# Batch 3 of a linear-attention and MLP kernel: its attention moved from four chunks into one slot, k of batch 4 mapped a group earlier, v and q of batch 4 loaded earlier

## The chip, the cores and the metric

The kernel runs on one core of a Trainium2 chip. The metric is the time of one execution on the device in microseconds (us), the median over several runs. An engine here is one of five units of the core that run their own instruction streams in order and wait for each other by semaphores: PE (matrix multiplies), DVE (vector), ACT (activation functions and copies), POOL (here: casts and fills at the start) and SP (here: it issues loads and transposing transfers). PEld is the part of PE that loads weights.

## The reference, cut to what matters

There are 8 batches of 8 heads, 576 tokens and 64 features. Linear attention is computed first, then a two-layer MLP over all 4608 tokens:

```python
phi = lambda x: np.where(x > 0, x, np.exp(x) - 1.0) + 1.0
q_p, k_p = phi(q), phi(k)
kv  = np.einsum('bhsd,bhse->bhde', k_p, v)
z   = np.sum(k_p, axis=2)
num = np.einsum('bhsd,bhde->bhse', q_p, kv)
den = np.einsum('bhsd,bhd->bhs', q_p, z)[..., None] + 1e-06
x   = (num / den) # heads side by side: 512 features a token
out = gelu_tanh(x @ w_in) @ w_out          # 512 -> 2048 -> 512
```

## The kernel before, in words

**Groups and slots.** The MLP runs in nine groups j = 0 to 8. Groups 0 to 7 take 512 tokens of batch j each; group 8 takes the 64 tokens that every batch has left over. `iteration(j)` (L741) writes out a group as 32 or more steps: 16 steps "h", each of four 128x512 matmuls (L388) and one gelu on ACT (L398), and then 16 steps "o" of four 128x512 matmuls (L725), which finish four output tiles t = 0 to 3. Group 1 has the order 8 h, 8 o, 8 h, 8 o, so that its four output tiles are finished in slots 28, 29, 30 and 31. After step number s of group j, `run(j, s)` emits whatever `at(j, s, ...)` had registered for that slot. This is the planner: attention work for later batches is written into slots of the MLP of earlier ones by hand. The tiling framework keeps the program's order on each engine and puts in the semaphore waits.

**What attention of batch b needs.** Loads of q, k, v (fp32) into a pool of seven slots that all inputs share in rotation; a load into a slot waits until the former tenant was read. `linear_of` (DVE, L230) makes x+1 clipped at 1; `exp_of` (ACT, L222) makes exp(x) into a buffer of which there is one for q and one for k; `least_of` (DVE, L236) takes the smaller of both, which is phi. ACT needs another function table for exp than for gelu, so each round of exps is followed by `gelu_table` (L411). `least_q` also issues four transposing transfers of phi(q) on SP's queue (qt, L632). `cast_v_paired` (DVE, L241) casts v beside a column of ones. `kv_paired` (L246, matmuls L252) makes kv with 72 matmuls of 64x64 by 65. Then come n = phi(q) times kv with its denominators (matmuls), `divide` (DVE, L285 and L286), and four transposing transfers of the result x (xt, L655), which are the input of group b's h steps.

**Two ways to make n.** Batches 1 to 3 use `nab` (L299): a chunk of 128 tokens takes four matmuls of 128x128 by 130 (L268) against kv in block-diagonal form (`kvbds`, zeroed once on POOL), and one divide of eight heads in a pair of PSUM banks. Batches 2 and 3 do this chunk by chunk in four slots of an h stage (`plan_by_chunks`, L659). Batches 4 to 7 use `nab_quads` (L312) in slot 17 of group b-1: 64 matmuls of 64x64 by 65 (L325) at one go, six result blocks of 65 columns to a bank, in four banks of the rotating pool and the pair; the two blocks that are left in the pair take kv of batch b+1 (L252), and its copy (L350) follows after the last divide. The kv of these batches is kept as plain blocks (`kvs`).

**PSUM.** Six banks rotate among h, o and n tiles; the pair of banks is separate.

**Around the change, before.** For batch 3: `linear_of` of q and k in slots 24 and 25 of group 1, the exps of q and k in slot 23, kv in slot 2 of group 2 (`kv_in_pair`, L637), n by chunks in slots 4, 6, 8 and 10 of group 2. For batch 4: k is loaded at (1, 10), q and v at (1, 29), both exps at (2, 15) together with that of k of batch 5, `least_q` at (2, 17), the cast of v at (2, 20), and kv alone in slot 2 of group 3. For batch 5: k is loaded at (2, 11), q and v at (2, 23). The output tiles t = 0 and 2 of a group are copied out of PSUM by DVE, t = 1 and 3 by ACT (L686), and ACT issues the two stores of a group (L714) between its copies.

Of the kernel before, what the change touches and what calls it, by code (L numbers as in the profile page):

```python
# [9 lines left out]
BF16 = mybir.dt.bfloat16  # L10
# [5 lines left out]
def kernel(  # L16
# [16 lines left out]
    nc = tc.nc  # L33

    B, H, S, D = q.shape
    d_model, d_ff = moe_w_in.shape
    P = 128
    HP = P // 2
    C = 4
    MAIN = P * C  # L40
    REST = S - MAIN
    NP = H // 2
# [3 lines left out]
    E = D + 1  # L46
# [15 lines left out]
    pkv = ctx.enter_context(tc.tile_pool(name="pkv", bufs=1))  # L62
# [26 lines left out]
    def ld_tile(name, b):  # L89
        shape = [P, H, C * D] if name == "q" else [P, NP, J * D]  # L90
        ld[name, b] = pld.tile(shape, FP32, name=name + "_x", tag="ld")
# [10 lines left out]
    def load_q(b):  # L102
        ld_tile("q", b)
        nc.sync.dma_start(
            out=ld["q", b],
            in_=q[b, :, 0:MAIN, :].rearrange("h (p c) d -> p h (c d)", c=C),
        )

    def load_all_pairs(name, src, b):
        ld_tile(name, b)  # L110
        load_pairs(name, src, b)
# [6 lines left out]
                in_=q[2 * m + s, :, MAIN:S, :].rearrange("h p d -> p h d"),  # L118
            )

    def load_batch(b):
        load_q(b)
        load_all_pairs("k", k, b)
        load_all_pairs("v", v, b)

    w_st = {}

    def load_w_in(i, parts=1):
# [46 lines left out]
    load_w_out(2, slice(2, 4))  # L175
    load_w_out(3, slice(0, 2))
    load_w_out(3, slice(2, 4))
    load_batch(2)
    load_batch(3)

# [1 line left out]
    nc.vector.memset(warm, 0.0)  # L184
    make_identity(nc, ident)
    vps = [pkv.tile([P, J * NP, E], BF16, name=f"vp{i}") for i in range(2)]
    kvbds = [pkv.tile([P, NP, 2 * E], BF16, name=f"kvbd{i}") for i in range(4)]
    kvs = [pkv.tile([P, NP, E], BF16, name=f"kv{i}") for i in range(4)]
    for i in range(2):
        nc.gpsimd.memset(vps[i][:, :, D:E], 1.0)  # L190
    for t in kvbds:
# [23 lines left out]
    def exp_of(name, b, hs=None):  # L215
        x = ld[name, b]
        hs = hs or slice(0, x.shape[1])
        if (name, b) not in exps:
            e = name + ("_e" if name != "qr" or b % 2 else "_f")
            exps[name, b] = pe.tile([P, x.shape[2] // D, x.shape[1], D], BF16, name=e)  # L220
        o, i = maps_view(name, b, x, exps[name, b], hs)
        nc.scalar.activation(o, i, AF.Exp)  # L222
# [17 lines left out]
    def cast_v_paired(b, us, fn):  # L240
        fn(  # L241
            out=vp_paired(b)[:, :, us, 0:D].rearrange("p j u d -> p u j d"),
            in_=ld["v", b][:, us].rearrange("p u (j d) -> p u j d", d=D),
        )
# [30 lines left out]
    def kv_of_head(b, s, i):  # L275

        r = slice(HP * s, HP * (s + 1))
        return kvs[b % 4][r, i, :] if b > 3 else kvbds[b][r, i, E * s : E * (s + 1)]

    def divide(x_v, n_v):  # L280

# [11 lines left out]
    def x_tile():  # L293
        return px.tile([P, d_model], BF16, name="x")
# [4 lines left out]
    def nab(qt_c, b):  # L299
        x, n_ps = x_tile(), pair_of_banks("n_ps")  # L300
        nab_mm(qt_c, kvbds[b], [n_ps[:, a] for a in range(2)])
        divide(by_parity(x), n_ps[:, :, 0 : 4 * E].rearrange("p a (u e) -> p a u e", e=E))
        return x
# [8 lines left out]
    def nab_quads(qt_cs, bs, kv_b):  # L312

        ns = [[bank("n_ps", [P, 6 * E]) for _ in range(2)] for _ in range(2)]
        n_pair = pair_of_banks("n_ps")
        ns.append([n_pair[:, s] for s in range(2)])
        units = [(c, i, a) for c in range(C) for i in range(2) for a in range(2)]
        for n, (c, i, a) in enumerate(units):  # L320
            g = n // 6
            for t in range(2):
                for s in range(2):
                    cs = slice(HP * t, HP * (t + 1))
                    nc.tensor.matmul(  # L325
                        ns[g][s][cs, E * (n - 6 * g) : E * (n - 6 * g + 1)],
                        lhsT=qt_cs[c][HP * s : HP * (s + 1), 2 * a + i, cs],
                        rhs=kv_of_head(bs[c][t], s, 2 * a + i),
                        skip_group_check=True,
                    )  # L330
        if kv_b is not None:
            for ii in range(2):
                kv_paired(kv_b, ii, lambda a, ii: n_pair[:, a, E * (4 + ii) : E * (5 + ii)])

        def x_of(transposed):
            x = pxs.tile([P, C, d_model], BF16, name="xs")
            x_v = x.rearrange("p c (i s a d) -> p s (c i) a d", s=2, a=2, d=D)
            for g in range(2):
                for s in range(2):
                    divide(  # L340
                        x_v[:, s, 3 * g : 3 * (g + 1)],
                        ns[g][s].rearrange("p (k a e) -> p k a e", a=2, e=E),
                    )
                for c in ((0,), (1, 2))[g]:
                    transposed(c, x[:, c])
            n_v = n_pair[:, :, 0 : 4 * E].rearrange("p s (k a e) -> p s k a e", a=2, e=E)
            divide(x_v[:, :, 6:8], n_v)
            transposed(3, x[:, 3])
            if kv_b is not None:
                nc.vector.tensor_copy(  # L350
                    out=kvs[kv_b % 4].rearrange("p (a i) e -> p a i e", a=2),
                    in_=n_pair[:, :, 4 * E : 6 * E].rearrange("p a (i e) -> p a i e", e=E),
                )

        return x_of
# [24 lines left out]
            nc.tensor.transpose(t_ps[:, n, :], x[:, P * i : P * (i + 1)], ident)  # L380
        fn(out=xt_c[:, blocks.start : blocks.stop], in_=t_ps)

    xts = {}
    qts = {}

    def h_mm(h_ps, xt, m, ts=slice(0, MAIN), blocks=range(KM)):
        for c in blocks:
# [118 lines left out]
    def at(j, slot, fn, *args):  # L506


        fill.setdefault((j, slot), []).append((fn, args))
# [68 lines left out]
        at(0, 35, h_begin, b, 0, slice(0, 3 * P))  # L578
        at(0, 35, h_begin, b, 0, slice(3 * P, MAIN))

    def plan_prepare(b, s_linear, s_exp):
        def casts():
            cast_v_paired(b, slice(0, NP), nc.vector.tensor_copy)

        def exps_all():
            for n in "qk":
                exp_of(n, b)

        j, s = s_linear
        for i, n in enumerate("qk"):  # L590
            at(j, s + i, linear_of, n, b)
        at(j, s + (7 if b == 4 else 2), casts)
        j, s = s_exp
        at(j, s, exps_all)
        at(j, s + 2, least_q, b)
        at(j, s + 4, least_of, "k", b)

    def plan_prepare_late(b):

        j = b - 3  # L600
        if b == 5:
            at(j, 15, exp_of, "k", b)
            at(j, 22, linear_of, "k", b)
        else:
            at(j, 12, linear_of, "k", b)
        at(j + 1, 8 if b == 5 else 4, cast_v_paired, b, slice(0, NP), nc.vector.tensor_copy)
        at(j + 1, 13, linear_of, "q", b)
        at(j + 1, 15, exp_of, "q", b)
        if b > 5:
            at(j, 15, exp_of, "k", b)  # L610
        at(j + 1, 20, least_q, b)
        at(j, 22, least_of, "k", b)

    def plan_rest(m):
        j = 5 + m // 2
# [21 lines left out]
    def kv_in_pair(b):  # L637
        kv_ps = pair_of_banks("kv_ps")
        for ii in range(2):
            kv_paired(b, ii, lambda a, ii: kv_ps[:, a, E * ii : E * (ii + 1)])  # L640
        src = kv_ps[:, :, 0 : 2 * E].rearrange("p a (i e) -> p a i e", e=E)
        if b > 3:
            nc.vector.tensor_copy(out=kvs[b % 4].rearrange("p (a i) e -> p a i e", a=2), in_=src)
        else:
            for s in range(2):
                r = slice(HP * s, HP * (s + 1))
                nc.vector.tensor_copy(
                    out=kvbds[b][r, :, E * s : E * (s + 1)].rearrange("p (a i) e -> p a i e", a=2),
                    in_=src[r],
                )  # L650

    def transposed_x(b, c, x):
        if b not in xts:
            xts[b] = pt.tile([P, NP, MAIN], BF16, name="xt")
        nc.sync.dma_start_transpose(out=xt_chunk(b, c), in_=x)  # L655

    rest_qt = {}

    def plan_by_chunks(b, j, s_kv, s_n):  # L659
        def n(c):  # L660
            transposed_x(b, c, nab(qts[b][:, c], b))

        at(j, s_kv, kv_in_pair, b)
        for c in range(C):
            at(j, s_n + 2 * c, n, c)

    def plan_attention(b):

# [105 lines left out]
            run(j, slot)  # L774

    plan_second()
    plan_prepare(2, (1, 2), (1, 7))
    at(1, 7, gelu_table)
    plan_by_chunks(2, 1, 16, 18)
    plan_by_chunks(3, 2, 2, 4)  # L780
    at(1, 10, load_all_pairs, "k", k, 4)
    plan_prepare(3, (1, 24), (1, 23))
    at(1, 23, gelu_table)
    at(1, 29, load_q, 4)
    at(1, 29, load_all_pairs, "v", v, 4)
    at(2, 11, load_all_pairs, "k", k, 5)
    at(2, 23, load_q, 5)
    at(2, 23, load_all_pairs, "v", v, 5)
    at(3, 2, kv_in_pair, 4)
    plan_prepare(4, (2, 13), (2, 15))  # L790
    for b in range(5, B):
        plan_prepare_late(b)
    for m in range(C):
        plan_rest(m)
    for b in range(4, B + 1):
        plan_attention(b)
    for b in range(6, B):
        at(b - 3, 1, load_all_pairs, "k", k, b)
        at(b - 3, 1, load_q, b)
        at(b - 3, 1, load_all_pairs, "v", v, b)  # L800
# [38 lines left out]
```

## Time and profile before

| what | us |
|---|---|
| median of 4 runs (284.19 to 284.82) | 284.64 |
| the profiled execution | 284.82 |
| its span, first instruction to last | 283.0 |
| PE busy | 277.2 |
| ACT busy | 164.5 |
| DVE busy | 103.2 |
| POOL busy | 15.5 |

How to read it: the span is what the instructions of the core cover; 1.8 us of the profiled execution lie around it. Busy time of one engine lies beside that of the others, so the column does not add up to the span. A matmul is shown with its full latency (379 ns for a 128x512 one), but the next one starts long before it ends; the space from start to start is what a matmul costs PE.

### The profile page before, as it was taken

Reading aid. Unit: us, or ns where it says so; the run is one execution under the profiler, and the core shown is the slowest. Engines: PE = TensorE matmul, PEld = TensorE weight load, DVE = VectorE, ACT = ScalarE, POOL = GpSimd, SP = SyncE. Lnnn points to the kernel's source line nnn. Section 1 sums busy time; section 2 is a strip of 40 time slices with the busy share of each in tenths; the row PEclk is TensorE's granted clock in tenths of the full one; section 3 lists DMA queues with packets and bytes.
Section 4 is the critical chain, followed back from the end, with each engine's and each line's share of the span. In section 5 each row is a group of like instructions: output and inputs, shape, how many; then the busy total and the mean of one; then the engine's idle time right before and its main releaser. Section 6 shows DMA issues by size and latency. Waiting matters only on the chain.

```text
span 283.0 us, 5377 instructions
## 1 busy us (share of the span) xinstructions
PE 277.2 (98%) x2293; PEld 135.9 (48%) x2293; DVE 103.2 (36%) x176; ACT 164.5 (58%) x224; POOL 15.5 (5%) x22
## 2 busy tenths in 40 slices
PE   8899999999999999999999999999999999999995
PEld 3484455445454444454445444544444444444444
DVE  2850286435856280286124650260115001400001
ACT  4768878785966955692468336832682264026400
POOL 4047200000000000000000000000000000000000
PEclk9999999999999999999999999999999999999999
DMA  6999999977899849966894660056505300420022
GB/s 234 400 407 396 411 401 404 402 254 209 90 207 332 225 90 330 398 226 167 172 393 111 164 132 0 2 148 142 120 2 139 120 2 0 138 87 0 0 76 74
DMA packets 59591, 53.83 MB, mean 190 GB/s; under 512 B 35760, under 2 KB 45360, under 8 KB 59568
## 3 DMA queue, kind: packets, MB, share of 16 engines
q1 hardware_dynamic: 56784, 44.58, 52.1%
q10 hardware_dynamic: 2784, 8.91, 8.5%
q8 instruction: 18, 0.29, 0.4%
q14 instruction: 5, 0.04, 0.0%
HBM read 36.70 MB, written 9.44 MB: 163 GB/s over the span
## 4 chain that ended last, share of the span: by engine, by line
PE 94%; DMA 3%; SPq 1%; DVE 1%; issue 0%; ACT 0%
PE o_ps L725 44%; PE h_ps L388 44%; DMA v_x<-in_v_dram 3%; PE n_ps L325 1%; PE kv_ps L252 1%; PE n_ps L268 1%; PE n_ps L252 1%; PE t_ps L380 1%; SPq L95 1%; SPq L100 0%; PE t_ps L534 0%; DVE vp L241 0%; DVE x L370 0%; DVE kvbd L264 0%; DVE o_sb L686 0%
## 5 line engine op out<-in xcount | busy, mean ns | idle before, releaser
L725 PE MATMUL o_ps<-w_out_sb,g 128*128 128x512 bf16 (+2 forms) x608 | 128.2, 368 | 0.0
L388 PE MATMUL h_ps<-xt,w_in_sb 128*128 128x512 bf16 (+1 forms) x564 | 114.6, 359 | 0.0
L398 ACT ACTIVATE g<-h_ps 128x512 bf16<-128x512 f32 x144 | 84.7, 599 | 38.9 <-PE h_ps L388 36.7
L388 PEld LDWEIGHTS <-w_in_sb 128*128 128x128 bf16 x628 | 58.3, 98 | 63.5
L725 PEld LDWEIGHTS <-g 128*128 128x128 bf16 x608 | 57.5, 98 | 63.6
L686 ACT COPY o_sb<-o_ps 128x512 f32<-128x512 f32 (+1 forms) x19 | 10.8, 576 | 61.8 <-PE o_ps L725 53.9
L686 DVE COPY o_sb<-o_ps 128x512 f32<-128x512 f32 (+1 forms) x19 | 12.2, 644 | 47.8 <-PE o_ps L725 42.9
L285 DVE RECIPROCAL r<-n_ps 128x6 f32<-128x6 f32 (+2 forms) x42 | 8.1, 193 | 55.5 <-PE n_ps L325 45.8
L222 ACT ACTIVATE k_e<-k_x 128x2304 bf16<-128x2304 f32 (+1 forms) x9 | 17.1, 1901 | 2.4 <-DVE k_p L236 1.4
L222 ACT ACTIVATE q_e<-q_x 128x2048 bf16<-128x2048 f32 (+1 forms) x9 | 15.5, 1721 | 3.4 <-DMA q_x<-in_q_dram 3.3
L230 DVE TENSOR_SCALAR k_p<-k_x 128x2304 bf16<-128x2304 f32 (+1 forms) x9 | 11.0, 1221 | 17.0 <-DMA k_x<-in_k_dram 17.0
L286 DVE TENSOR_TENSOR xs<-n_ps,r 128x384 bf16<-128x384 f32 (+1 forms) x25 | 14.6, 584 | 0.9
L230 DVE TENSOR_SCALAR q_p<-q_x 128x2048 bf16<-128x2048 f32 (+1 forms) x9 | 9.9, 1102 | 13.5 <-DMA q_x<-in_q_dram 13.5
L236 DVE TENSOR_TENSOR q_p<-q_p,q_e 128x2048 bf16<-128x2048 bf16 (+1 forms) x9 | 9.9, 1101 | 11.7 <-ACT q_e L222 11.6
L388 PE MATMUL h_ps<-xt_rest,w_in_sb 128*128 128x512 bf16 x64 | 14.0, 379 | 0.0
L241 DVE CAST vp<-v_x 128x2304 bf16<-128x2304 f32 (+1 forms) x9 | 11.0, 1226 | 7.2 <-DMA v_x<-in_v_dram 7.0
L411 ACT ACT_TABLE_LOAD x9 | 11.5, 1283 | 0.2
L236 DVE TENSOR_TENSOR k_p<-k_p,k_e 128x2304 bf16<-128x2304 bf16 (+1 forms) x9 | 11.0, 1221 | 1.3 <-ACT k_e L222 1.0
L420 PE MATMUL w_ps<-warm 128*128 128x512 bf16 x32 | 10.2, 478 | 1.2 <-DVE warm L184 1.2
L286 DVE TENSOR_TENSOR x<-n_ps,r 128x512 bf16<-128x512 f32 (+1 forms) x17 | 10.7, 628 | 0.6
L222 ACT ACT_TABLE_LOAD x8 | 10.3, 1283 | 0.1
L144 POOL CAST w_in_sb<-w_st 128x512 bf16<-128x512 f32 (+2 forms) x6 | 7.6, 1269 | 14.9 <-DMA w_st<-in_moe_w_in_dram 14.9
(50 smaller groups left out, 79.7 us busy)
## 6 DMA issues: line engine op xcount, KB each, us to landing
out_dram<-o_sb ACTq DMA_DIRECT2D x16, 512.0 KB, 3.1
k_x<-in_k_dram SPq DMA_DIRECT2D x7, 1152.0 KB, 11.5
v_x<-in_v_dram SPq DMA_DIRECT2D x7, 1152.0 KB, 12.9
q_x<-in_q_dram SPq DMA_DIRECT2D x6, 1024.0 KB, 12.7
w_st<-in_moe_w_in_dram SPq DMA_DIRECT2D x3, 1024.0 KB, 13.6
q_x<-in_q_dram SPq DMA_DIRECT2D x4, 512.0 KB, 8.9
w_st<-in_moe_w_out_dram SPq DMA_DIRECT2D x2, 1024.0 KB, 12.5
w_st<-in_moe_w_out_dram SPq DMA_DIRECT2D x4, 512.0 KB, 11.2
```

The costliest lines, as they stand in the source:

```text
L222: nc.scalar.activation(o, i, AF.Exp)
L230: nc.vector.tensor_scalar(o, i, 1.0, 1.0, op0=ALU.add, op1=ALU.max)
L236: nc.vector.tensor_tensor(p, p, e, op=ALU.min)
L241: fn(out=vp_paired(b)[:, :, us, 0:D].rearrange("p j u d -> p u j d"), in_=ld["v", b][:, us].rearrange("p u (j d) -> p u j d", d=D),)
L285: nc.vector.reciprocal(r, n_v[heads + (D,)])
L286: nc.vector.tensor_tensor(x_v, n_v[heads + (slice(0, D),)], r[heads + (None,)].to_broadcast(shape + [D]), op=ALU.mult,)
L388: nc.tensor.matmul(h_ps[:, ts], lhsT=w_in_sb[:, c, P * m : P * (m + 1)], rhs=xt[:, c, ts], start=(c == 0), stop=(c == KM - 1), skip_group_ ...
L398: nc.scalar.activation(g[:, m, :], h_ps, AF.Gelu_apprx_tanh)
L411: nc.scalar.preload_act_table_set("gelu_apprx_tanh_and_others")
L420: nc.tensor.matmul(w_ps, lhsT=warm[:, 0:P], rhs=warm)
L686: (nc.scalar.copy if on_scalar else nc.vector.tensor_copy)(dst, src)
L725: nc.tensor.matmul(o_ps, lhsT=g[:, m, P * t : P * (t + 1)], rhs=w_out_sb[:, m, fs], start=(m == 0), stop=(m == MM - 1),)
```

## The change

Batch 3 is planned as batches 4 to 7 were. Its n is made by `nab_quads` in slot 17 of group 2, with kv of batch 4 in the two blocks left over, and no longer in four chunks in slots 4 to 10; kv of batch 4 no longer stands alone in slot 2 of group 3. For that, phi of k of batch 4 has to be ready before slot 17 of group 2: its exp stands in slot 23 of group 1 behind those of k and q of batch 3 (k is now first), its `linear_of` and `least_of` in slots 5 and 6 of group 2, and the cast of v of batch 4 moves to (2, 10), `least_q` of batch 4 to (2, 20). The kv of batch 3 itself moves from slot 2 to slot 4 of group 2 and is kept as plain blocks; a fourth block-diagonal buffer and its fill on POOL go. v and q of batch 4 are loaded at (1, 26), now ahead of the transposing transfers of batch 3's q on SP's queue; k, q and v of batch 5 at (2, 1). `kvs` gets a buffer of its own for each of batches 3 to 7. The planning functions are renamed; for batch 2 and batches 5 to 7 the slots are those of before, but for linear of k of batch 5 (now (2, 14)) and the cast of v of batch 5 (now (3, 4)).

```diff
-    kvbds = [pkv.tile([P, NP, 2 * E], BF16, name=f"kvbd{i}") for i in range(4)]
-    kvs = [pkv.tile([P, NP, E], BF16, name=f"kv{i}") for i in range(4)]
+    kvbds = [pkv.tile([P, NP, 2 * E], BF16, name=f"kvbd{b}") for b in range(3)]
+    kvs = {b: pkv.tile([P, NP, E], BF16, name=f"kv{b}") for b in range(3, B)}
...
-        return kvs[b % 4][r, i, :] if b > 3 else kvbds[b][r, i, E * s : E * (s + 1)]
+        return kvs[b][r, i, :] if b > 2 else kvbds[b][r, i, E * s : E * (s + 1)]
...
+    def plan_fourth():
+
+        for name, b in (("k", 3), ("q", 3), ("k", 4)):
+            at(1, 23, exp_of, name, b)
+        at(1, 23, gelu_table)
+        at(1, 24, linear_of, "k", 3)
+        at(1, 25, linear_of, "q", 3)
+        at(1, 26, least_of, "k", 3)
+        at(1, 31, least_q, 3)
+        at(2, 0, cast_v, 3)
+        at(2, 4, kv_in_pair, 3)
+        at(2, 5, linear_of, "k", 4)
+        at(2, 6, least_of, "k", 4)
+
+    def plan_prepare(j):
+
+        b = j + 2
+        has_k = b + 1 < B
+        at(j, 10 if j == 2 else 4, cast_v, b)
+        if has_k:
+            at(j, 14 if j == 2 else 12, linear_of, "k", b + 1)
+        at(j, 13, linear_of, "q", b)
+        at(j, 15, exp_of, "q", b)
+        at(j, 20, least_q, b)
+        if has_k:
+            at(j, 15, exp_of, "k", b + 1)
+            at(j, 22, least_of, "k", b + 1)
...
-        if b > 3:
-            nc.vector.tensor_copy(out=kvs[b % 4].rearrange("p (a i) e -> p a i e", a=2), in_=src)
+        if b > 2:
+            nc.vector.tensor_copy(out=kvs[b].rearrange("p (a i) e -> p a i e", a=2), in_=src)
...
-    plan_by_chunks(3, 2, 2, 4)
     at(1, 10, load_all_pairs, "k", k, 4)
-    plan_prepare(3, (1, 24), (1, 23))
-    at(1, 29, load_q, 4)
-    at(1, 29, load_all_pairs, "v", v, 4)
-    at(2, 11, load_all_pairs, "k", k, 5)
-    at(2, 23, load_q, 5)
-    at(2, 23, load_all_pairs, "v", v, 5)
-    at(3, 2, kv_in_pair, 4)
-    plan_prepare(4, (2, 13), (2, 15))
...
-    for b in range(4, B + 1):
+    for b in range(3, B + 1):
         plan_attention(b)
-    for b in range(6, B):
+    at(1, 26, load_all_pairs, "v", v, 4)
+    at(1, 26, load_q, 4)
+    for b in range(5, B):
         at(b - 3, 1, load_all_pairs, "k", k, b)
         at(b - 3, 1, load_q, b)
         at(b - 3, 1, load_all_pairs, "v", v, b)
```

More of the change, by code (lines that the diff above doesn't have):

```diff
@@ L119, in load_rest @@
             )
[L121 to L124, printed above, removed]
     w_st = {}
@@ L177 @@
     load_w_out(3, slice(2, 4))
-    load_batch(2)
-    load_batch(3)
+    for b in (2, 3):
+        load_q(b)
+        load_all_pairs("k", k, b)
+        load_all_pairs("v", v, b)
     warm = const.tile([P, 512], BF16, name="warm")
@@ L350, in x_of @@
                 nc.vector.tensor_copy(
-                    out=kvs[kv_b % 4].rearrange("p (a i) e -> p a i e", a=2),
+                    out=kvs[kv_b].rearrange("p (a i) e -> p a i e", a=2),
                     in_=n_pair[:, :, 4 * E : 6 * E].rearrange("p a (i e) -> p a i e", e=E),
@@ L381, in transpose_x @@
         fn(out=xt_c[:, blocks.start : blocks.stop], in_=t_ps)
-    xts = {}
-    qts = {}
+    xts, qts, rest_qt = {}, {}, {}
     def h_mm(h_ps, xt, m, ts=slice(0, MAIN), blocks=range(KM)):
@@ L579, in plan_second @@
         at(0, 35, h_begin, b, 0, slice(3 * P, MAIN))
[L581 to L612, printed above, removed]
+    def cast_v(b):
+        cast_v_paired(b, slice(0, NP), nc.vector.tensor_copy)
@@ new lines, in plan_third, with n @@
+    def plan_third():
+        def n(c):
+            transposed_x(2, c, nab(qts[2][:, c], 2))
+        for i, name in enumerate("qk"):
+            at(1, 2 + i, linear_of, name, 2)
+            at(1, 7, exp_of, name, 2)
+        at(1, 4, cast_v, 2)
+        at(1, 7, gelu_table)
+        at(1, 9, least_q, 2)
+        at(1, 10, load_all_pairs, "k", k, 4)
+        at(1, 11, least_of, "k", 2)
+        at(1, 16, kv_in_pair, 2)
+        for c in range(C):
+            at(1, 18 + 2 * c, n, c)
+    def plan_fourth():
[10 more added lines that the diff above has]
+        at(2, 6, least_of, "k", 4)
@@ L655, in transposed_x @@
         nc.sync.dma_start_transpose(out=xt_chunk(b, c), in_=x)
[L657 to L665, printed above, removed]
     def plan_attention(b):
@@ L776 @@
     plan_second()
-    plan_prepare(2, (1, 2), (1, 7))
-    at(1, 7, gelu_table)
-    plan_by_chunks(2, 1, 16, 18)
-    plan_by_chunks(3, 2, 2, 4)
-    at(1, 10, load_all_pairs, "k", k, 4)
-    plan_prepare(3, (1, 24), (1, 23))
-    at(1, 23, gelu_table)
-    at(1, 29, load_q, 4)
-    at(1, 29, load_all_pairs, "v", v, 4)
-    at(2, 11, load_all_pairs, "k", k, 5)
-    at(2, 23, load_q, 5)
-    at(2, 23, load_all_pairs, "v", v, 5)
-    at(3, 2, kv_in_pair, 4)
-    plan_prepare(4, (2, 13), (2, 15))
-    for b in range(5, B):
-        plan_prepare_late(b)
+    plan_third()
+    plan_fourth()
+    for j in range(2, 6):
+        plan_prepare(j)
     for m in range(C):
         plan_rest(m)
-    for b in range(4, B + 1):
+    for b in range(3, B + 1):
         plan_attention(b)
-    for b in range(6, B):
+    at(1, 26, load_all_pairs, "v", v, 4)
+    at(1, 26, load_q, 4)
+    for b in range(5, B):
         at(b - 3, 1, load_all_pairs, "k", k, b)
```

## The prediction

> **What bounds the kernel now.** I read the page first: busy times, then the chain that ended last.
>
> ```profile
> PE 277.2 (98%) x2293; PEld 135.9 (48%) x2293; DVE 103.2 (36%) x176; ACT 164.5 (58%) x224; POOL 15.5 (5%) x22
> ...
> PE 94%; DMA 3%; SPq 1%; DVE 1%; issue 0%; ACT 0%
> ```
>
> PE is busy 98% of the span and 94% of the chain runs on it. A busy PE could still be stretched, because a matmul's record is its latency; so I took the timeline of PE for the stretch that the change touches (start, duration, what, count), and read it from start to start.
>
> ```profile
> 77.39 2.75 PE L388 MATMUL h_ps<-xt,w_in_sb 128*128 128x512 bf16 x12
> 80.07 0.78 PE L252 MATMUL kv_ps<-vp,k_p 64*64 64x65 bf16 x72
> 80.78 1.90 PE L388 MATMUL h_ps<-xt,w_in_sb 128*128 128x512 bf16 x8
> 82.52 0.40 PE L268 MATMUL n_ps<-kvbd,qt 128*128 128x130 bf16 x4
> 82.76 1.89 PE L388 MATMUL h_ps<-xt,w_in_sb 128*128 128x512 bf16 x8
> ...
> 106.76 2.75 PE L388 MATMUL h_ps<-xt,w_in_sb 128*128 128x512 bf16 x12
> 109.45 0.78 PE L252 MATMUL kv_ps<-vp,k_p 64*64 64x65 bf16 x72
> 110.16 11.40 PE L388 MATMUL h_ps<-xt,w_in_sb 128*128 128x512 bf16 x52
> 121.39 1.89 PE L725 MATMUL o_ps<-w_out_sb,g 128*128 128x512 bf16 x8
> 123.21 0.76 PE L325 MATMUL n_ps<-kv,qt 64*64 64x65 bf16 x64
> 123.79 0.86 PE L252 MATMUL n_ps<-vp,k_p 64*64 64x65 bf16 x72
> 124.58 0.60 PE L725 MATMUL o_ps<-w_out_sb,g 128*128 128x512 bf16 x2
> ```
>
> Between 110.16 and 121.39, 52 big matmuls take 11.23 us: 0.216 each. From 77.39 (h of group 2) to 121.39 (end of h of group 3) lie 44.00 us with 64+64+64 = 192 big matmuls, 41.43 us at 0.2158 (the o stage's 64 from 92.95 to 106.76). The rest, **2.57 us**, is attention; no wait is left in it. So in this stretch time goes only with PE's own work, unless the change makes PE wait.
>
> **The change on PE, step by step.**
> - Removed: n of batch 3. Four chunks, each from its first matmul to the next h (82.52 to 82.76): 0.24, in all 0.96 (0.94 by three more digits).
> - Removed: kv of batch 4 alone. 106.76 to 110.16 is 3.40 for 12 big matmuls (2.59) and the 72 small ones: 0.81, of which some 0.09 is the passage from full-array matmuls to 64x64 ones.
> - Moved by two slots: kv of batch 3, 77.39 to 80.78, 3.39 - 2.59 = 0.80 before and after.
> - Added: 64 matmuls of L325 and the 72 of kv in one slot. The trace shows it for batch 4: 121.39 to 124.58 is 3.19 with 8 big matmuls (1.73), so 1.46, again with 0.09 for the one passage.
>
> Before 0.80 + 0.95 + 0.81 = 2.56; after 0.80 + 1.46 = 2.26. **PE gains 0.30 us**: 64 quarter-array matmuls take 0.58 where 16 full ones took 0.95 (9 ns each), and the kv of batch 4 loses its own passage but not its 72 matmuls.
>
> A rule that speaks against this: the Trainium skill, "TensorE: Matmul & The Clock Gate", section "Wait — 56ns, not 53.3ns?", says that matmuls never start closer than about 25 ns apart, however small. The 64 would then be some 1.6 us, an estimate from that page, and the change would lose 0.7 us. The row of 123.21 (64 in 0.58) decides against it for 64x64 tiles, and the sum does not use it.
>
> **What lies beside PE, and its slack.** DVE loses four divides of 0.21+0.69 and gains four of 0.19+0.56 and one of 0.20+0.69, and is 36% busy; POOL loses one fill of 0.5 us at 1.4 to 3.5 us and then waits for a load until 13.55. Both at nothing. If DVE were late with the divides of slot 17, the first to wait would be the third output tile 24 big matmuls later (5 us). The tight place is ACT at the end of group 1:
>
> ```profile
> 71.06 1.28 ACT L222 ACT_TABLE_LOAD   x1
> 72.36 1.91 ACT L222 ACTIVATE q_e<-q_x 128x2048 bf16<-128x2048 f32 x1
> 74.18 2.11 ACT L222 ACTIVATE k_e<-k_x 128x2304 bf16<-128x2304 f32 x1
> 76.30 1.28 ACT L411 ACT_TABLE_LOAD   x1
> 77.59 0.59 ACT L686 COPY o_sb<-o_ps 128x512 f32<-128x512 f32 x1
> 79.23 0.37 ACTq L714 DMA_DIRECT2D out_dram<-o_sb  x1
> 79.70 0.58 ACT L686 COPY o_sb<-o_ps 128x512 f32<-128x512 f32 x1 [1.52 <-PE h_ps L388]
> 80.31 0.34 ACTq L714 DMA_DIRECT2D out_dram<-o_sb  x1
> 80.70 1.08 ACT L398 ACTIVATE g<-h_ps 128x512 bf16<-128x512 f32 x2 [0.42 <-ACT o_sb L686]
> ```
>
> The exp of k of batch 4 goes between the second exp and the table load. It adds a wait: there is one buffer for exp(k), which `least_of` of k of batch 3 must have read. DVE, free at 72.40, does linear k (1.35), linear q (1.22), then `least_of` k (1.35): done at 76.15, when ACT is done with its two exps (76.29). So almost no wait; k of batch 4 itself is there (issued 65.58, 5.8 us to landing: 71.4). Then: exp to 78.4, table to 79.7, first copy to 80.3, store, second copy to 81.3, store, gelu of h step 0 at 81.7 to 82.3, against 80.70 now. Queued behind the exp are these copies and gelus, and for them waits PE. Its dates in group 2, from 77.39 in steps of 0.863: the built order gives banks so that h step 2 and 3 wait for DVE's copies (done by 77.5, early, since the copies now stand before `least_q` and the cast, where they were at 78.47 to 79.75), h step 4 (80.85) for ACT's first copy (80.3: **0.55 us of slack**), h step 5 (82.5, after kv) for the second (81.3), step 6 (83.4) for the first gelu (82.3). From there a gelu (0.53 to 0.60) is faster than an h step. So I cost this at nothing; each 0.1 us beyond the slack costs 0.1.
>
> A rule weighed here: the Trainium skill, "ScalarE: Activation LUTs", section "What ACT_TABLE_LOAD costs", puts a switch at about 2.66 us, of which 1.38 is a drain. Then the first copy would end 1.4 later and h step 4 would wait some 0.8, an estimate from that page: +0.5 in all. The rows show 1.28 and the copy 0.01 after it; they decide, and the sum leaves it out.
>
> **SP's queue and the loads.** v and q of batch 4 now go out when the fourth xt transfer of batch 2 is issued, at 73.7 (before: 82.3 and 83.2), ahead of the qt transfers of batch 3 (least_q done at 78.7, needed at 93.9 in slot 17). The xt transfers stay ahead; the last lands 2.4 after 72.50, before 77.39. k, q and v of batch 5 follow the qt transfers at 84, land between 90 and 99, and are needed at 88 to 91 (linear k, DVE, harmless to 5 us as above) and later. xt of batch 3 now leaves at 96 to 101; batch 4's left 2 us after its n as well (125.19 against 123.21) and its h stage did not wait.
>
> One wait is new and cannot be read from the source: in the built order ACT's second store of group 1 waits for a semaphore that the load of v of batch 4 raises when it lands (before: an xt transfer's). Behind this store stand all gelus of group 2. It must have landed by 82.3. I take the row of the k load at 65.58, which like it followed qt or xt transfers alone, 5.8 (k at 92.34, same place: 5.9): 79.6, slack 2.7. The other loads give bounds: v at 83.22 9.1, v at 104.52 12.9, v at 108.26 17.5, all queued behind other loads, which this one is not.
>
> **Sum.** -0.30 on PE, the rest hidden. The profiled execution's 284.82 (span 283.0 and 1.8 around) would be 284.52; it lies 0.18 above the median, so I forecast 284.64 - 0.30 = **284.34**, a change of 0.1%. About 0.2% (0.57 us) is what a measurement of this kernel can tell from no change.
>
> **The rivals.**
> - *ACT late for the bank of h step 4* (the change does nothing for the time): the two waits between DVE and ACT cost 0.85 instead of nothing, 0.3 beyond the slack, and eat the gain: 284.6. For: 0.55 is little. Against: all rows in it are measured here. At 1.4 beyond it is 285.7. 12%.
> - *The load of v holds the second store* (slower): decides from a landing later than 8.6 us. With 9.1 PE loses 0.5: 284.8. With 12.9 the load lands at 86.6, gelu 0 ends at 87.7 and h step 6 waits 4.3: 288.6; with 17.5 it is 293. For: queue times in this trace reach 17.5. Against: nothing big is ahead of it. 6%.
> - *Faster than PE's sum*: if batch 3's stage hid a stall that my start-to-start reading takes for work. The 2.57 us leave no room beyond 0.05, so only the spread of the runs (0.45 below the median) brings 283.9. 7%.
>
> The forecast has 75%. Range 283.9 to 285.3: from the spread below to a stall of 1 us; what is left out is a load that takes over 9.6 us. Within 0.2% (284.07 to 285.21) fall the forecast but for 2% of spread, two thirds of the first rival and a third of the second (the load at 9.1): 0.82 with rounding; faster 0.09; slower 0.09.
>
> **What would show it.** Right: n of batch 3 as 64 matmuls in 0.58 at about 93.8 us, big matmuls 0.216 apart around it, and the h stage of group 3 ended at 121.09 where it now ends at 121.39. The exp of k of batch 4 at 76.3, first copy ended by 80.3, gelu 0 at 81.7. Wrong: a gap before h step 4, 5 or 6 of group 2 (80.9, 82.5, 83.4), named after ACT's copy or gelu; a second store issued later than 81.4; DVE's linear of k of batch 5 later than 97.

## The result and the profile after

| | before | after |
|---|---|---|
| median, us (lowest to highest) | 284.45 (284.17 to 284.82), 53 runs | 284.16 (283.88 to 284.53), 33 runs |
| the profiled execution | 284.82 | 284.20 |
| its span | 283.0 | 282.4 |

The ratio after to before is 0.9989, with a 95% interval of 0.9984 to 0.9994: a gain of 0.31 us by the ratio (0.17 to 0.46) and of 0.29 by the medians, where 0.30 was forecast. It is measurable over many runs, and lies inside the 0.2% that the prediction took as no change.

From the page of the changed kernel, the span, the busy times and the chain that ended last: the engines' shares are those of before and the chain is still 94% PE. PE is busy for 1.2 us less (277.2 before), but that is not the gain: half of it, 0.6, lies in the first 13 us, ahead of the change.

```profile
span 282.4 us, 5465 instructions
...
PE 276.0 (98%) x2341; PEld 135.2 (48%) x2341; DVE 102.6 (36%) x177; ACT 164.1 (58%) x224; POOL 15.0 (5%) x21
...
PE 94%; DMA 3%; SPq 1%; DVE 1%; issue 0%; ACT 0%
```

The timeline of PE in the changed kernel, for the stretch shown of before (start, duration, engine, line, operation, tiles, count):

```profile
77.09 4.48 PE L384 MATMUL h_ps<-xt,w_in_sb 128*128 128x512 bf16 x20
81.50 0.78 PE L249 MATMUL kv_ps<-vp,k_p 64*64 64x65 bf16 x72
82.21 9.67 PE L384 MATMUL h_ps<-xt,w_in_sb 128*128 128x512 bf16 x44
91.72 1.89 PE L725 MATMUL o_ps<-w_out_sb,g 128*128 128x512 bf16 x8
93.54 0.76 PE L322 MATMUL n_ps<-kv,qt 64*64 64x65 bf16 x64
94.12 0.86 PE L249 MATMUL n_ps<-vp,k_p 64*64 64x65 bf16 x72
94.92 12.26 PE L725 MATMUL o_ps<-w_out_sb,g 128*128 128x512 bf16 x56
107.01 13.98 PE L384 MATMUL h_ps<-xt,w_in_sb 128*128 128x512 bf16 x64
120.83 1.89 PE L725 MATMUL o_ps<-w_out_sb,g 128*128 128x512 bf16 x8
```

No line carries a wait. From 91.72 to 94.92 is 3.194 us by one more digit of the starts, with eight big matmuls (1.726): the merged slot costs 1.47, of which the 64 matmuls of n take 0.58 (93.54 to 94.12). Group 3's h stage runs through (107.01 to 120.83) with no kv in it.

**Where to set the ruler.** The two spans differ by 0.6, twice the effect. The other 0.3 comes before the change has begun. In the timelines of PE at the start, the first kv matmuls wait for DVE, which casts v of batch 0 in two halves; the second of these casts starts 0.02 after its load has landed (12.15 before, 11.91 after). Before:

```profile
12.11 0.48 PE L252 MATMUL kv_ps<-vp,k_p 64*64 64x65 bf16 x36 [0.51 <-DVE vp L241]
```

and after:

```profile
11.88 0.48 PE L249 MATMUL kv_ps<-vp,k_p 64*64 64x65 bf16 x36 [0.51 <-DVE vp L238]
```

That is 0.23 earlier in this one execution, and the h stage of group 2 starts 0.30 earlier (77.09 against 77.39). From that start to the end of group 3's h stage it was 44.00 us (121.39 - 77.39) and is 43.73 (120.83 - 77.09, by one more digit): -0.27. From the start of the first o matmul of the kernel to that of the last matmul of all it was 248.76 and is 248.44: -0.32. The 0.05 between the two is a wait in group 0, where kv of batch 1 follows eight o matmuls and needs DVE's cast of v (ended at 40.21 before, 39.90 after); before:

```profile
38.41 1.89 PE L725 MATMUL o_ps<-w_out_sb,g 128*128 128x512 bf16 x8
40.27 0.78 PE L252 MATMUL kv_ps<-vp,k_p 64*64 64x65 bf16 x72
```

and after:

```profile
38.16 1.89 PE L725 MATMUL o_ps<-w_out_sb,g 128*128 128x512 bf16 x8
39.98 0.78 PE L249 MATMUL kv_ps<-vp,k_p 64*64 64x65 bf16 x72
```

From start to start that is 1.87 before (by one more digit) and 1.82 after. It isn't the change's: it is 1.87 again in the last of the experiments on ACT (1024 columns), which is built on the changed kernel, and 1.82 in the other runs built on it. So the stretch of 43.73, and not the span, is to be set beside the 0.30: 0.27 of it is PE's.

The timeline of ACT around the end of group 1, in the changed kernel (what it waited for stands in brackets):

```profile
70.77 1.28 ACT L219 ACT_TABLE_LOAD   x1
72.06 2.13 ACT L219 ACTIVATE k_e<-k_x 128x2304 bf16<-128x2304 f32 x1
74.09 1.89 ACT L219 ACTIVATE q_e<-q_x 128x2048 bf16<-128x2048 f32 x1
75.89 2.11 ACT L219 ACTIVATE k_e<-k_x 128x2304 bf16<-128x2304 f32 x1
78.03 1.28 ACT L407 ACT_TABLE_LOAD   x1
79.32 0.59 ACT L686 COPY o_sb<-o_ps 128x512 f32<-128x512 f32 x1
79.94 0.34 ACTq L714 DMA_DIRECT2D out_dram<-o_sb  x1
80.37 0.58 ACT L686 COPY o_sb<-o_ps 128x512 f32<-128x512 f32 x1 [0.47 <-ACT o_sb L686]
80.99 0.35 ACTq L714 DMA_DIRECT2D out_dram<-o_sb  x1
81.38 3.04 ACT L394 ACTIVATE g<-h_ps 128x512 bf16<-128x512 f32 x6 [0.42 <-ACT o_sb L686]
```

The three exps stand close together, so the single buffer of exp(k) cost no wait. This execution is 0.30 ahead of the one before, so 0.30 is added to compare: exp of k of batch 4 at 76.2, first copy ended at 80.2, first gelu at 81.7. The forecast had 76.3, 80.3 and 81.7. PE wanted the bank of that first copy at 77.09 + 4 x 0.863 = 80.54; it was free at 79.91. **The slack is 0.63.**

### The profile page after: what moved, and what is told of

Same layout as the page of the kernel before. It is cut to its first block, busy times and chain, and to the rows that moved or that the text cites. A ratio compares the mean times of both kernels' runs of the same rounds, so it can differ in the third digit from the quotient of the medians.

```text
span 282.4 us, 5465 instructions
## 1 busy us (share of the span) xinstructions
PE 276.0 (98%) x2341; PEld 135.2 (48%) x2341; DVE 102.6 (36%) x177; ACT 164.1 (58%) x224; POOL 15.0 (5%) x21
## 4 chain that ended last, share of the span: by engine, by line
PE 94%; DMA 3%; SPq 1%; DVE 1%; issue 0%; ACT 0%
PE o_ps L725 44%; PE h_ps L384 44%; DMA v_x<-in_v_dram 3%; PE n_ps L322 1%; PE n_ps L249 1%; PE kv_ps L249 1%; PE n_ps L265 1%; PE t_ps L377 1%; SPq L95 1%; SPq L100 0%; PE t_ps L530 0%; DVE vp L238 0%; DVE x L367 0%; DVE kvbd L261 0%; DVE o_sb L686 0%
## 5 line engine op out<-in xcount | busy, mean ns | idle before, releaser
L283 DVE TENSOR_TENSOR xs<-n_ps,r 128x384 bf16<-128x384 f32 (+1 forms) x30 | 17.5, 584 | 1.0
L416 PE MATMUL w_ps<-warm 128*128 128x512 bf16 x32 | 9.1, 436 | 1.2 <-DVE warm L181 1.2
L283 DVE TENSOR_TENSOR x<-n_ps,r 128x512 bf16<-128x512 f32 (+1 forms) x13 | 7.9, 609 | 0.4
```

The costliest lines, as they stand in the source:

```text
L283: nc.vector.tensor_tensor(x_v, n_v[heads + (slice(0, D),)], r[heads + (None,)].to_broadcast(shape + [D]), op=ALU.mult,)
L416: nc.tensor.matmul(w_ps, lhsT=warm[:, 0:P], rhs=warm)
```

## The experiments

The theory: the gain is PE's own work alone (n in quarter-array matmuls -0.16, kv of batch 4 without a slot of its own -0.13), and all that was moved is hidden as long as ACT's chain at the end of group 1 stays within some 0.6 us. Rivals: the gain comes from the loads that leave sooner, or from the fill on POOL that went; or ACT's chain has already eaten part of it. The kernel before, on the same chip as each experiment, gave 284.40 beside the first four and 284.39 beside the last three.

### n of batch 3 in quarter-array matmuls, kv of batch 4 alone again

Edit on the changed kernel:

```diff
-                x_of = nab_quads([qts[b][:, c] for c in range(C)], bs, b + 1 if b + 1 < B else None)
+                x_of = nab_quads([qts[b][:, c] for c in range(C)], bs, b + 1 if 3 < b < B - 1 else None)
...
+    at(3, 2, kv_in_pair, 4)
```

> One half of the change alone on PE: the changed kernel, but kv of batch 4 goes back to a slot of its own (slot 2 of group 3) and n of batch 3 stays as 64 small matmuls in slot 17 of group 2. Theory (the time is PE's own work, all else is hidden): n alone takes 0.09 + 0.70 as for batch 7 (210.50 to 211.19 in the trace of before), kv alone 0.81, so PE works 0.13 us longer than in the changed kernel and 0.16 shorter than before: 284.29, ratio to before 0.9994. Rival (the gain is all in the passage that kv of batch 4 no longer pays): as before, 284.45. Rival (the gain is not on PE but in the earlier loads or the start): as the changed kernel, 284.16. The medians are too close to part them alone; the starts of PE's groups in the trace decide, to 0.01 us.

Measured: 284.15 (284.07 to 284.48), ratio 0.9995 (0.9986 to 1.0003). The times can't part this from either kernel; the timeline of PE can:

```profile
91.49 1.89 PE L725 MATMUL o_ps<-w_out_sb,g 128*128 128x512 bf16 x8
93.31 0.76 PE L322 MATMUL n_ps<-kv,qt 64*64 64x65 bf16 x64
94.01 12.26 PE L725 MATMUL o_ps<-w_out_sb,g 128*128 128x512 bf16 x56
106.10 2.75 PE L384 MATMUL h_ps<-xt,w_in_sb 128*128 128x512 bf16 x12
108.79 0.78 PE L249 MATMUL kv_ps<-vp,k_p 64*64 64x65 bf16 x72
109.50 1.69 PE L384 MATMUL h_ps<-xt,w_in_sb 128*128 128x512 bf16 x7
```

n alone costs 94.01 - 91.49 - 1.73 = 0.79, against 0.95 in chunks; kv alone 109.50 - 106.10 - 2.59 = 0.81, against 0.68 as second in the merged slot (1.47 - 0.79). So -0.16 and -0.13 by the groups. From the start of group 2's h stage to the end of group 3's the three kernels take 44.00, 43.87 and 43.73: -0.13 and -0.14. (From first o matmul to last matmul it is 248.76, 248.57 and 248.44; the first step holds the 0.05 of group 0.) Both halves of the PE sum are there, and of about the same size.

The starts of single matmuls show what the merging saves. The passage into 64x64 tiles costs 0.09 (309 ns from the last big matmul to the first small one, against 216 between big ones), and the way back 0.12 (125 ns from the last small one to the first big one, against some 8 between small ones). The merged slot has one passage less each way, 0.21, but the 72 kv matmuls behind n spread over 0.67 from first to last start, against 0.59 alone; why they are slower there, the record doesn't show.

### Only the loads sooner

Edit on the kernel before (attention of batches 3 and 4 as it was):

```diff
-    at(1, 29, load_q, 4)
-    at(1, 29, load_all_pairs, "v", v, 4)
-    at(2, 11, load_all_pairs, "k", k, 5)
-    at(2, 23, load_q, 5)
-    at(2, 23, load_all_pairs, "v", v, 5)
+    at(1, 26, load_all_pairs, "v", v, 4)
+    at(1, 26, load_q, 4)
-    for b in range(6, B):
+    for b in range(5, B):
```

> The other part alone: the kernel before, with only the loads moved (v and q of batch 4 to slot 26 of group 1, k, q and v of batch 5 to slot 1 of group 2); batch 3 still in four chunks, k of batch 4 mapped as before. Theory: nothing on PE changes, 284.45, ratio 1.0000 within 0.0005, and PE's groups between 77 and 121 us have the same lengths as before. Rival (the earlier loads bring the gain): 284.16, ratio 0.9990.

Measured: 284.33 (284.15 to 284.71), ratio 0.9998 (0.999 to 1.0007); and the stretch from the start of group 2's h stage to the end of group 3's takes 44.00 us, as before. The loads give nothing by themselves. What they are for shows in the next experiment.

### The loads late

Edit on the changed kernel:

```diff
-    at(1, 26, load_all_pairs, "v", v, 4)
-    at(1, 26, load_q, 4)
+    at(1, 31, load_q, 4)
+    at(1, 31, load_all_pairs, "v", v, 4)
```

> The changed kernel with v and q of batch 4 loaded late again: q, then v, in slot 31 of group 1 behind the qt transfers of batch 3, about where they were before the change; k, q and v of batch 5 still at slot 1 of group 2 behind them. Theory (the earlier loads earn nothing themselves, but the merged slot needs them): v is issued at about 84 and lands 9 to 13 later (rows of before: 9.1 at 83.22, 12.9 at 104.52), 93 to 97; its cast takes 1.36; kv of batch 4, due at 94.1, waits 0.5 to 4.3 us. Time 284.7 to 288.5; likeliest 285 (9.1 to landing). Rival (loads are hidden wherever they stand): 284.16.

Measured: 285.56, ratio 1.0036 (1.0017 to 1.0055). The runs lie 2.25 us apart (284.46 to 286.71), those of the changed kernel 0.65. In the profiled execution (285.70), DVE's timeline has the cast of v of batch 4 waiting 8.67 us for its load:

```profile
94.29 1.36 DVE L238 CAST vp<-v_x 128x2304 bf16<-128x2304 f32 x1 [8.67 <-DMA v_x<-in_v_dram]
```

and PE's has the merged slot waiting behind it:

```profile
93.53 0.76 PE L322 MATMUL n_ps<-kv,qt 64*64 64x65 bf16 x64
95.70 0.77 PE L249 MATMUL n_ps<-vp,k_p 64*64 64x65 bf16 x72 [1.41 <-DVE vp L238]
96.41 1.90 PE L725 MATMUL o_ps<-w_out_sb,g 128*128 128x512 bf16 x8
```

From n to the next o matmuls it is 2.88 here and 1.38 in the changed kernel: +1.50, the excess of this execution (285.70 against 284.20). So moving kv of batch 4 forward by a group does put a due time on v, some 92.8 us (kv at 94.12 in the changed kernel, less the cast's 1.36), and the sooner load is the cover that the merge needs. That the spread of the runs is that of the load's landing is my reading; one execution was traced. A by-product: the divides of batch 3 ran 4.5 us later here, from 98.47 to 102.2, and the o matmuls after the slot, which started 1.5 later themselves, did not wait (56 in 12.10, as in the changed kernel). So some 3 us of the prediction's "5 us" of slack on DVE were used without cost.

### The exps in another order

Edit on the changed kernel:

```diff
-        for name, b in (("k", 3), ("q", 3), ("k", 4)):
+        for name, b in (("q", 3), ("k", 3), ("k", 4)):
```

> The changed kernel with the exp of q of batch 3 ahead of that of k again, as before the change; nothing else. The order of the exps decides when DVE can read exp(k), and with it when ACT may start the exp of k of batch 4. Theory (the slack before h step 4 of group 2 is what covers the third exp): least_of of k of batch 3 ends 1.3 us later (77.3 for 75.9 on the changed kernel's clock), exp of k of batch 4 runs 77.4 to 79.5, table to 80.8, first copy to 81.4; h step 4, due at 80.6, waits 0.8 us, steps 5 and 6 no more than that. Time 284.16 + 0.8 = 285.0, ratio to before 1.0018. Rival (ACT has slack to spare, order costs nothing): 284.16. A trace without a gap before h step 4 speaks against the theory.

Measured: 284.98 (284.82 to 285.25), ratio 1.002 (1.0012 to 1.0029), 0.82 above the changed kernel's median. The timeline of ACT:

```profile
73.57 2.11 ACT L219 ACTIVATE k_e<-k_x 128x2304 bf16<-128x2304 f32 x1
77.10 2.12 ACT L219 ACTIVATE k_e<-k_x 128x2304 bf16<-128x2304 f32 x1 [1.43 <-DVE k_p L233]
79.24 1.28 ACT L407 ACT_TABLE_LOAD   x1
80.54 0.59 ACT L686 COPY o_sb<-o_ps 128x512 f32<-128x512 f32 x1
```

and of PE:

```profile
76.78 3.62 PE L384 MATMUL h_ps<-xt,w_in_sb 128*128 128x512 bf16 x16
81.17 1.02 PE L384 MATMUL h_ps<-xt,w_in_sb 128*128 128x512 bf16 x4 [0.78 <-ACT o_sb L686]
82.13 0.78 PE L249 MATMUL kv_ps<-vp,k_p 64*64 64x65 bf16 x72
```

With k of batch 3 second, its exp ends at 75.7 and DVE reads the one buffer only after that; the third exp waits 1.43, the copy ends at 81.13, and h step 4, due at 76.78 + 3.45 = 80.23, starts at 81.17. From start to start 20 h matmuls take 5.35 against 4.41: 0.94 lost, which is 81.17 - 80.23. The rival "ACT late for the bank of h step 4" is real and stands where it was put; the order of the three exps is what keeps it away.

### How much slack ACT has: half a microsecond more, one more

Both edits add to the changed kernel an exp of 512 (or 1024) columns of k of batch 4 into a tile that nobody reads, behind the three exps; this is work that the reference does not ask for.

```diff
+        spare = const.tile([P, 512], BF16, name="spare")        # 1024 in the second
+        at(1, 23, lambda: nc.scalar.activation(
+            spare, ld["k", 4][:, 0:1].rearrange("p u f -> p (u f)")[:, 0:512], AF.Exp))
         at(1, 23, gelu_table)
```

> The changed kernel with one more exp of 128x512 into a spare tile behind the exp of k of batch 4: 0.5 us more work on ACT ahead of its first copy of group 1. In the changed kernel's trace that copy ends at 79.91 and h step 4 of group 2 starts at 80.55; e3 shows the step 0.04 after the copy, so the slack is 0.60. Theory (cover with an edge): 0.51 to 0.60 more is just covered, no gap before h step 4 over 0.05, time 284.16. Rival (every us on ACT before the copies counts): 284.7.

> The same with a 128x1024 exp, about 1.0 us more on ACT (rows: 128x1024 takes 1.06 at 5.11, some 0.09 of it beside its neighbour). Theory: 1.0 - 0.6 = 0.4 us gap before h step 4 of group 2, time 284.56, and copy 2 and gelu 0 add none. Rival (ACT's cover is wide): 284.16. Rival (all of it counts): 285.2.

Measured: with 512 columns 284.16 (284.0 to 284.52), ratio 0.999 (0.9981 to 0.9999), 20 h matmuls in 4.41 as without; the copy ended at 80.61 and step 4 started on time, at 80.73. The first copy on ACT and the h matmuls on PE in that kernel:

```profile
80.02 0.59 ACT L693 COPY o_sb<-o_ps 128x512 f32<-128x512 f32 x1
77.27 4.48 PE L384 MATMUL h_ps<-xt,w_in_sb 128*128 128x512 bf16 x20
```

With 1024 columns 284.54 (284.33 to 284.74), ratio 1.0005 (0.9996 to 1.0014). That kernel's timelines, ACT:

```profile
77.78 1.04 ACT L603 ACTIVATE spare<-k_x 128x1024 bf16<-128x1024 f32 x1
78.84 1.28 ACT L407 ACT_TABLE_LOAD   x1
80.14 0.59 ACT L693 COPY o_sb<-o_ps 128x512 f32<-128x512 f32 x1
```

and PE:

```profile
76.96 3.62 PE L384 MATMUL h_ps<-xt,w_in_sb 128*128 128x512 bf16 x16
80.77 1.02 PE L384 MATMUL h_ps<-xt,w_in_sb 128*128 128x512 bf16 x4 [0.20 <-ACT o_sb L693]
```

The copy ended at 80.73 and h step 4 started 0.04 later, at 80.77, 0.36 after its due time; the median is 0.38 above that with 512 columns. The bracket's 0.20 is less than the loss, since it counts only the time in which no matmul's latency was running. So the half microsecond is free, the full one costs what is beyond the slack, and the gain of the change is gone.

### The fill on POOL restored

Edit on the changed kernel:

```diff
-    for t in kvbds:
+    kvbd_spare = pkv.tile([P, NP, 2 * E], BF16, name="kvbd_spare")
+    for t in kvbds + [kvbd_spare]:
         nc.gpsimd.memset(t, 0.0)
```

> The changed kernel with the fourth fill on POOL put back (of a buffer that nothing reads). The profiled execution of the changed kernel reached its first kv matmuls 0.23 us earlier than that of before (11.88 for 12.11), which the prediction did not count. Theory (that is the spread between executions; the fill lies under a wait for a load): as the changed kernel, 284.16, ratio to before 0.9989. Rival (the fill that went is part of the gain): 284.4, ratio to before 0.9997.

Measured: 284.09 (284.0 to 284.44), ratio 0.9992 (0.9983 to 1.0); first o matmul to last matmul 248.44, as in the changed kernel. The fill is no part of the gain, and the earlier start of the changed kernel's profiled execution does not come from it: here kv of batch 0 starts at 11.81, with the fill.

## Why the prediction was right

- *PE's sum*: 2.56 before and 2.26 after were forecast. Measured, 0.80 for kv of batch 3 (20 h matmuls start to start in 4.41, then 0.71 to the next) and 1.47 for the merged slot: 2.27. All prices were rows of the kernel before, the merged one from batch 4, whose work has the same shape. The 0.30 is some 0.02 too large by rounding alone: with one more digit the same rows give 2.55 and 2.27. The stretch shows 0.27, in two halves of 0.13 and 0.14. The reason given for the second half was too simple: "its own passage but not its 72 matmuls" would be 0.09. It is a passage in and one back, 0.21, less 0.08 for slower kv matmuls. The sum came out because the merged slot was priced whole, from a row, and not put together from its parts.
- *The rule on matmul starts*: the 64 matmuls of 64x64 took 0.58 again, 9.0 ns each, in batch 3's place too. The figure of the Trainium skill, "TensorE: Matmul & The Clock Gate", section "Wait — 56ns, not 53.3ns?", does not hold for these tiles; the estimate that went with it (+0.7) did not come.
- *ACT's chain*: forecast within 0.1 us at each step. Slack 0.55 forecast, 0.63 seen; the two added exps enclose it: the copy ended 0.52 later at no cost, and 0.95 later at a cost of 0.36. The two reasons given for a free wait held: the exps' order (reversed, it cost 0.94) and the table load at 1.28. The copy stands 0.01 behind the table load here too, so the drain that the Trainium skill's "ScalarE: Activation LUTs", section "What ACT_TABLE_LOAD costs", adds to it is not seen in this place.
- *The load of v*: issued at 73.72 as forecast, it landed 5.9 later, at 79.6, against 5.8 and 79.6. ACT's second store went out at 80.99, 0.04 after its copy, so it did not wait for it. The rival's price was not measured: in the one run that loads v later, this store waits for the semaphore of an xt transfer instead. What a late v does by its other road, through the cast and kv, is +1.5 in the traced execution.
- *k of batch 5* was called late but harmless: in the changed kernel DVE waited 3.16 us for it before 91.22, and nothing followed on PE.
- *xt of batch 3* was issued from 95.52 on (forecast 96 to 101) and group 3 began with no wait.
- *What was missing*: the prediction took its own time by taking 0.30 from the median of four runs, 284.64. Over 53 runs that median is 284.45, so the changed kernel came out at 284.16 and not 284.34. The difference was right to 0.01 us (0.30 against 0.29 by the medians), which is luck to that digit: the interval spans 0.17 to 0.46, and PE's share is 0.27. The level was 0.18 too high; the working itself noted a spread of the runs as large as the effect, but took the four at their word.

## What to carry to other kernels

When one engine is the bound and has no gaps, price a rearrangement by its start-to-start groups, with the passage between kinds of tiles, there and back, as a term of its own, and take the merged price from a place in the same trace where the merged form already runs. Then write down the due time of each thing that was moved (a PSUM bank, a load, a single buffer) and its slack: here the gain of 0.3 us rested on 0.6 us of slack on ACT and on a load of v placed ahead of a queue of transfers, and the loss of either turned the sign. For effects this small compare stretches of the trace and not spans.

## What the runs showed that was not expected

- The start of the kernel varies more than the change is worth. In nine profiled executions the first kv matmuls start between 11.57 and 12.11 us; that 0.54 is most of the spread of the runs before (284.17 to 284.82). It goes with the landing of the first loads (the second half of v of batch 0 landed at 12.15 in the latest of these executions, at 11.59 in the earliest), and not with what the kernels change. The kernel with only the loads moved, whose PE work is that of before, shows it: its first kv matmuls start 0.38 earlier (11.73 against 12.11), and its profiled execution is 0.38 shorter (284.44 against 284.82). After that PE's stretches repeat to 0.01 us where nothing waits.
- PE's passage from 128x128 to 64x64 tiles costs 0.09 us each time in the stretch (before kv, before the merged slot, before n alone), and the way back 0.12; between n and kv, both in 64x64, there is none to be seen.
- The load of v of batch 4, issued at 86.02 us behind the transposing transfers and the load of q, landed 8.2 us later in the traced execution with late loads, against 5.9 when issued at 73.72; being late on the queue cost twice in that execution, in the start and in the length.
